# Weight sums and token splits moved in the order of a transform and dense-layer kernel

## The chip, the cores and the metric

The kernel runs on one core of one Trainium2 chip. The metric is the device time of one execution in microseconds (us). TensorE is called PE here, VectorE DVE, ScalarE ACT, GpSimd POOL, and the queue that issues most transfers SP, as in the profile.

## The reference

What is computed is attention over 4 x 8 heads of 576 rows with a bias from a small network on the distance of two rows, then on its output `x` (4 batches, 576 rows, 512 columns) the real part of a Fourier transform over rows and columns, a normalisation and two dense layers:

```python
attn = exp(scores - max) / (sum + 1e-9);  x = attn @ v          # heads joined: (4, 576, 512)
X = np.fft.fft(np.fft.fft(x, axis=1), axis=2)
u = x + np.real(X)
un = (u - mean(u)) / np.sqrt(var(u) + 1e-6)
return u + np.maximum(un @ w_ch1, 0.0) @ w_ch2                  # 512 -> 2048 -> 512
```

## The kernel before

Each float32 operand of the dense layers and of the transform is kept as a high part (a copy rounded to a shorter mantissa, written by ACT) and a low part (the rest, a subtraction on DVE or POOL). A product is three matmul passes: high by high, high by low, low by high (`PROD`, L606). So every operand that reaches PE costs one ACT copy and one subtraction first (`split`, L936; `split_sum`, L1166).

Work is tiled in 128 rows. After attention, batches 0 and 1 run through `dense` (L948): for each of 16 slices f of the hidden layer, `layer(f)` (L987) makes the parts of the two weights, multiplies the tokens by the first weight (`up`, L966, into a PSUM tile `hp`) and makes the parts `hh` and `hl` of the positive part (`relu_parts`); `down(f)` (L995) multiplies by the second weight and adds into `acc`. Of the 30 pieces of batch 1, `main[-1]` is `layer(15)`, `main[-2]` is `down(13)`, and `last_down` is `down(14)` and `down(15)`.

While batch 1 runs, batches 2 and 3 are transformed in a list of steps (`BETWEEN`, L74). Letters are looked up in `step` (L1356): `f12` is the last feature transform (matmuls into the two PSUM tiles `abp`), `i12` an ACT copy of one of them (`bs`), and `j12` (`join`, L708) the last sums, two DVE instructions that write `dm` (L713) and `dp` (L714) from the other. `w` calls `pr.weights(0)` (L1171), see below. The lower half of `x` is added from `dm` by POOL (L727), the upper from `dp` by DVE (L724).

Batches 2 and 3 then run as a pair (`class Pair`, L1108) with a seven-product scheme in the style of Strassen: sums of tokens (operands "3" to "7", `second_low`, L1157) times sums of weights. `weights(i)` loads two weight slices into a room of its own, makes four sums on DVE (L1180, tiles `ws`), and returns `weight_parts(i)` (L1188), which splits them: ACT copies `w1h` (L939), `wo` (L1200 twice, L1204) and POOL subtractions (L940, L1201 twice, L1205). `split_sum` makes the parts of one token sum, 128 x 1024 elements: an ACT copy (L1168) and a subtraction on the engine named in its call (L1169). `product(i, n, bank)` (L1208) issues six matmuls into bank a, b, x or y; a and b take their PSUM buffers from the pool `hps`, of two buffers, which also holds `hp` of `up(14)` and `up(15)`. `product(0, "1", "a")` takes the first of them again and `product(0, "6", "b")` the second.

What sets the order: at this stage PE is in the order written (`manual_schedule(engines={PE_})`, L1384), and so is DVE (L899, to the end). ACT, POOL and SP are ordered by a planner at build time, which simulates the program, and gives an idle engine the ready instruction that stands first in the program. In `first_layers` (L1259) four ACT instructions have a written order of their own among themselves: the copy of bank a (L1268), then the high parts of "5", "7" and "4".

In the block at L1384 PE runs `main[-10]`, the first flips (transposes `ut`, L1125, into the pool `fps` of two buffers, which `abp` also used) of row tiles 0 and 1, `main[-9]`, the flips of tiles 2 and 3, and so on. On DVE, between them, stand the statistics (`stats`, L761) and `first_low` (L1135), which frees the flips' buffers.

Of the kernel before, what the change touches and what calls it, by code (L numbers as in the profile page):

```python
# [13 lines left out]
AF = mybir.ActivationFunctionType  # L14
# [60 lines left out]
p000 p001 p002 g00 p010 h00 z000 z001 a000 a001 p011 p012 g01 b000 b001 h01 z010 z011 a010 a011  # L75
p100 p101 p102 g10 b010 b011 f00 i00 h10 p110 j00 l00 k00 f01 i01 p111 p112 g11 j01 l01 k01 h11
z100 z101 a100 a101 m00 m01 b100 b101 z110 z111 a110 a111 m02 m03 b110 b111 f10 i10 r0 d00 d01
j10 f11 i11 l10 k10 d02 d03 R j11 f12 i12 l11 k11 w j12
""".split()


# [56 lines left out]
def body(ctx, tc, a, out):  # L138
    nc = tc.nc
# [68 lines left out]
    def prep(n):  # L208
        q, k = ld.pop(n)
        qs = stp.tile([P, 2 * S], F32R, tag="qs", name="qs")  # L210
        kh = stp.tile([P, KW], F32R, tag="kh", name="kh")
        kl = stp.tile([P, KW], F32R, tag="kl", name="kl")
        stk[n] = (qs, kh, kl)

        def hi(dst, src, c):
            if n < 2:
                nc.scalar.activation(dst[:, c], src[:, c], AF.Copy)
            else:
                nc.gpsimd.tensor_scalar(dst[:, c], src[:, c], 1.0, 0.0, ALU.mult, ALU.add)  # L219

        def lo(dst, src, ref, rows, c):
            eng = nc.vector if n < 2 else nc.gpsimd
            eng.tensor_tensor(dst[rows, c], src[rows, c], ref[rows, c].bitcast(F32), ALU.subtract)  # L223

        every, low = slice(0, 128), slice(64, 128)
        ca, cb, ck = slice(0, S), slice(S, 2 * S), slice(S, KW)
        return [
            lambda: hi(qs, q, ca), lambda: lo(qs, q, qs, low, ca),
            lambda: hi(kh, k, ca), lambda: lo(kl, k, kh, every, ca),
            lambda: hi(qs, q, cb), lambda: lo(qs, q, qs, low, cb),  # L230
            lambda: hi(kh, k, ck), lambda: lo(kl, k, kh, every, ck),
        ]
# [93 lines left out]
    with ExitStack() as st:  # L326
# [51 lines left out]
        ps = None  # L378
# [16 lines left out]
        for n, (u, t4, rev, low, _) in enumerate(steps):  # L395
# [13 lines left out]
            if t4 == 0:  # L409
                ps = bps.tile([P, 2, 512], F32, tag="ps", name="bps")  # L410
# [15 lines left out]
    with ExitStack() as st:  # L426
# [137 lines left out]
        PE_, DVE_, ACT_, POOL_ = (getattr(mybir.EngineType, e) for e in ("PE", "DVE", "Activation", "Pool"))  # L564
# [23 lines left out]
        for n in range(U - 1):  # L588
            pr = prep(n + 1) if n else []
# [35 lines left out]
        class Mix:  # L625
# [95 lines left out]
            def add(self, t, upper):  # L721
                for pr, bo, bi, tt, lo, hi in self.d[t]:
                    if upper:
                        nc.vector.tensor_tensor(  # L724
                            x[pr, bo, tt, 257:512], x[pr, bi, tt, 257:512], hi[pr, 255:0:-1], ALU.add)
                    else:
                        nc.gpsimd.tensor_tensor(x[pr, bo, tt, 0:257], x[pr, bi, tt, 0:257], lo[pr], ALU.add)  # L727
# [91 lines left out]
        n = U - 1  # L819
# [82 lines left out]
        for w in TAIL:  # L902
            u = n - w.count("'")
            w = w.rstrip("'")
# [20 lines left out]
        def w1_pair(j):  # L925
            return w1p.tile([P, 2, 4 * P], F32, tag=f"w1_{(j + 3) % 8}", name="w1")
# [6 lines left out]
        def w1_load(f, dst=None):  # L933
            nc.sync.dma_start(w1[f] if dst is None else dst, w1_d[f].rearrange("p k c -> p (k c)"))
# [173 lines left out]
        class Pair:  # L1108
# [150 lines left out]
            def first_layers(self, last_down):  # L1259

                add = lambda d, p, q: nc.vector.tensor_tensor(d, p, q, ALU.add)
                ps = self.ps = {}
                u2 = rawp.tile([P, 2, 512], F32, tag="raw", name="us")
                c21 = rawd.tile([P, 2, 512], F32, tag="raw", name="us")
                last_down[0]()
                self.product(0, "1", "a")
                with tc.manual_schedule(engines={ACT_}):
                    nc.scalar.activation(u2[:, 0], ps["a"], AF.Copy)  # L1268
                    for n, eng in (("5", nc.vector), ("7", nc.gpsimd), ("4", nc.gpsimd)):
                        self.split_sum(n, eng)  # L1270
                self.product(0, "6", "b")
                add(u2[:, 0], ps["b"], u2[:, 0])
                last_down[1]()
                self.product(0, "5", "y")
                self.product(0, "7", "x")
                add(u2[:, 1], ps["x"], u2[:, 0])
                self.product(0, "2", "a")
                add(self.hc[1], ps["y"], u2[:, 1])
                self.weights(1)[1]()
                self.halves(0, ps["a"])  # L1280
                self.product(0, "4", "x")
                add(c21[:, 0], ps["x"], u2[:, 0])
                self.product(0, "3", "y")
                add(self.hc[0], ps["y"], u2[:, 0])
                self.w2_get(0)
                self.halves(1, c21[:, 0])
# [65 lines left out]
        pr = Pair(2)  # L1352
# [27 lines left out]
        def each(fn, *ts):  # L1380
            for t in ts:
                fn(t)

        with tc.manual_schedule(engines={PE_}):  # L1384
            main[-10]()
            each(first, 0, 1)
            each(stats, 0, 2)
            each(pr.first_low, 0, 1)
            main[-9]()
            each(first, 2, 3)  # L1390
            each(stats, 1, 3)
            each(pr.first_low, 2, 3)
            main[-8]()
            main[-7]()
            root()
            each(scale, 0, 1, 2, 3)
            pr.late_rooms()
            main[-6]()
            main[-5]()
            parts[1]()  # L1400
            each(flip, 0, 1)
            each(pr.second_low, 0, 1)
            mx[1].add(2, False)
            mx[1].add(2, True)
            main[-4]()
            main[-3]()
            each(flip, 2, 3)
            each(pr.second_low, 2, 3)
            pr.upper_parts(0, parts[0])
            main[-2]()  # L1410
            pr.split_sum("6", nc.vector)
            main[-1]()
            pr.run_first(last_down, end)
            un, stats, root, scale = norm(rest_tiles, lambda: pp.tile([P, 2, 512], F32, tag="p", name="un", bufs=4))
            room = []

            def rest_flip(t):
                if not room:
                    room.append(pp.tile([P, 2, 4, 256], F32R, tag="p", name="uo", bufs=4))
                ps = tps.tile([P, 4, P], F32, tag="t", name="ut")  # L1420
                c = slice(P * t, P * t + P)
                for kb in range(4):
                    nc.tensor.transpose(ps[:, kb], un[0][:, t, P * kb:P * kb + P], ident)
                h, l = room[0][:, 0, :, c], room[0][:, 1, :, c]
                nc.scalar.activation(h, ps, AF.Copy)
                nc.vector.tensor_tensor(l, ps, h.bitcast(F32), ALU.subtract)

            def w1_again(j):
                t = w1_pair(j)
                for e in range(2):  # L1430
                    w1[2 * j + e] = t[:, e]
                    w1_load(2 * j + e)

            extra = {f: [lambda j=f - 2: w1_again(j)] for f in range(2, 10)}
            for f, p in ((3, lambda: stats(0)), (4, lambda: stats(1)), (5, root), (6, lambda: scale(0)),
                         (7, lambda: scale(1)), (10, lambda: rest_flip(0)), (11, lambda: rest_flip(1))):
                extra.setdefault(f, []).append(p)
            pr.run_second(extra)
# [69 lines left out]
```

## Time and profile before

| what | us |
|---|---|
| median of the timed runs | 757.22 |
| fastest timed run | 757.07 |
| the profiled execution, whole | 757.49 |
| its span, first to last instruction | 755.7 |
| around the span (757.49 - 755.7) | 1.8 |

A row of the timeline gives the start, the time taken, engine and line, operation, output and inputs, the shape, how many instructions were merged (x), and in brackets how long the engine stood idle before it and what ended that.

### The profile page before, as it was taken

Reading aid. Unit: us, or ns where it says so; the run is one execution under the profiler, and the core shown is the slowest. Engines: PE = TensorE matmul, PEld = TensorE weight load, DVE = VectorE, ACT = ScalarE, POOL = GpSimd, SP = SyncE. Lnnn points to the kernel's source line nnn. Section 1 sums busy time; section 2 is a strip of 40 time slices with the busy share of each in tenths; the row PEclk is TensorE's granted clock in tenths of the full one; section 3 lists DMA queues with packets and bytes.
Section 4 is the critical chain, followed back from the end, with each engine's and each line's share of the span. In section 5 each row is a group of like instructions: output and inputs, shape, how many; then the busy total and the mean of one; then the engine's idle time right before and its main releaser. Section 6 shows DMA issues by size and latency. Waiting matters only on the chain.

```text
span 755.7 us, 13307 instructions
## 1 busy us (share of the span) xinstructions
PE 738.5 (98%) x4731; PEld 602.5 (80%) x4731; DVE 489.3 (65%) x1044; ACT 440.2 (58%) x912; POOL 347.6 (46%) x301
## 2 busy tenths in 40 slices
PE   6999999999999999999999999999999999999998
PEld 3567787888878888878888888878878888888897
DVE  7997584787687887794866476666474433354433
ACT  7997888788888788753333343344533342344453
POOL 0002654754465754125464445366864353344442
PEclk9999999999999999999999999999999999999999
DMA  8988889679479882265532221212242223642432
GB/s 220 240 218 210 197 228 277 184 198 299 124 205 255 240 263 84 89 207 170 167 112 84 61 80 29 69 38 62 70 140 58 69 83 98 204 152 78 139 91 78
DMA packets 62771, 110.85 MB, mean 147 GB/s; under 512 B 9232, under 2 KB 28304, under 8 KB 61584
## 3 DMA queue, kind: packets, MB, share of 16 engines
q1 hardware_dynamic: 58976, 102.13, 47.2%
q10 hardware_dynamic: 3440, 4.78, 1.9%
q0 software_dynamic: 288, 3.08, 1.1%
q8 instruction: 37, 0.61, 0.3%
q14 instruction: 30, 0.25, 0.1%
HBM read 86.24 MB, written 21.07 MB: 142 GB/s over the span
## 4 chain that ended last, share of the span: by engine, by line
PE 87%; ACT 4%; DMA 3%; SPq 2%; issue 1%; DVE 1%; POOL 1%; ACTq 0%; DVEq 0%; POOLq 0%
PE acc L999 14%; PE hp L974 14%; PE acc L1249 12%; PE s L282 11%; PE o L483 10%; PE t L462 8%; PE hpy L1218 3%; PE hpx L1218 3%; PE hpa L1218 3%; PE zp L681 2%; PE abp L701 2%; PE hpb L1218 1%; DMA bias<-ring 1%; ACT ha L390 1%; ACT ring L358 1%
## 5 line engine op out<-in xcount | busy, mean ns | idle before, releaser
L303 DVE CUSTOM_DVE_ANT_0 p<-s,bias 128x576 f32<-128x576 f32 x128 | 95.2, 754 | 54.9 <-PE s L282 50.0
L940 POOL TENSOR_TENSOR w2l<-w2f,w2h 128x512 fp32r<-128x512 f32 x64 | 85.1, 1329 | 92.5 <-ACT w2h L939 92.3
L940 POOL TENSOR_TENSOR w1l<-w,w1h 128x512 fp32r<-128x512 f32 x55 | 72.7, 1322 | 70.4 <-ACT w1h L939 68.1
L282 PE MATMUL s<-kh,qs 128*128 128x288 f32 (+1 forms) x320 | 98.2, 326 | 1.8 <-DVE nm L303 1.8
L442 ACT ACTIVATE pt<-t 128x512 f32<-128x512 f32 x141 | 77.8, 594 | 37.6 <-PE t L462 20.1
L318 ACT ACTIVATE p<-p,nm 128x576 f32<-128x576 f32 x128 | 98.0, 769 | 2.6 <-DVE nm L303 2.6
L282 PE MATMUL s<-kl,qs 128*128 128x288 f32 (+1 forms) x320 | 88.0, 294 | 0.8 <-DVE kl L223 0.8
L483 PE MATMUL o<-pt,v 128*64 128x288 f32 x640 | 84.2, 411 | 0.0
L219 POOL TENSOR_SCALAR kh<-kT 128x576 fp32r<-128x576 f32 (+1 forms) x28 | 20.7, 758 | 137.3 <-PE s L282 117.9
L939 ACT ACTIVATE w2h<-w2f 128x512 fp32r<-128x512 f32 x80 | 50.2, 627 | 56.1 <-PE acc L999 22.4
L462 PE MATMUL t<-ident,p 128*128 128x128 f32 x576 | 78.9, 273 | 0.7 <-ACT pt L442 0.7
L983 DVE SCALAR_TENSOR_TENSOR hl<-hp,hh 128x512 fp32r<-128x512 f32 (+1 forms) x48 | 28.9, 601 | 75.7 <-ACT hh L982 75.5
L939 ACT ACTIVATE w1h<-w 128x512 fp32r<-128x512 f32 x55 | 34.7, 632 | 65.8 <-PE hp L974 48.6
L282 PEld LDWEIGHTS s<-kh,qs 128*128 128x128 f32 (+1 forms) x320 | 58.5, 183 | 18.1 <-issue 7.4
L483 PEld LDWEIGHTS o<-pt,v 128*64 128x64 f32 x640 | 43.2, 137 | 30.8 <-issue 4.5
L462 PEld LDWEIGHTS t<-ident,p 128*128 128x128 f32 x576 | 66.5, 140 | 1.6 <-ACT pt L442 1.4
L999 PE MATMUL acc<-w2h,hh 128*128 128x512 f32 x160 | 62.7, 393 | 0.0
L999 PE MATMUL acc<-w2l,hh 128*128 128x512 f32 x160 | 62.4, 391 | 0.0
L282 PEld LDWEIGHTS s<-kl,qs 128*128 128x128 f32 (+1 forms) x320 | 58.8, 184 | 1.0 <-DVE kl L223 1.0
L999 PE MATMUL acc<-w2h,hl 128*128 128x512 f32 x160 | 59.5, 391 | 0.0
L412 PE MATMUL bps<-hd,sm 128*32 128x288 f32 x432 | 50.9, 420 | 7.5 <-DVE hd L392 5.3
L1249 PE MATMUL acc<-w2h,hh 128*128 128x512 f32 x128 | 50.0, 391 | 0.0
(200 smaller groups left out, 1771.6 us busy)
## 6 DMA issues: line engine op xcount, KB each, us to landing
w2f<-w_d SPq DMA_DIRECT2D x80, 256.0 KB, 2.6
raw<-m SPq DMA_DIRECT2D x24, 512.0 KB, 4.8
w<-w_d SPq DMA_DIRECT2D x45, 256.0 KB, 3.4
kT<-kT SPq DMA_DIRECT2D x32, 304.0 KB, 5.1
qT<-qT SPq DMA_DIRECT2D x32, 288.0 KB, 4.3
bias_d<-ring SPq DMA_DIRECT2D x54, 144.0 KB, 2.7
bias<-bias_d SPq DMA_DIRECT2D x24, 288.0 KB, 5.2
v<-v SPq DMA_DIRECT2D x16, 320.0 KB, 5.7
```

The lines of the kernel that those rows point to most:

```text
L282: nc.tensor.matmul(ps[:m, c, :CH], qs[:, c0:c0 + m], kk[:, k0 + c * CH:k0 + (c + 1) * CH], start=k == 0, stop=k == 1, skip_group_check=True)
L303: nc.vector.tensor_tensor_reduce(p, bank.pop((n, i))[:, :, :CH], bias, -0.125, 3.0e38, ALU.add, ALU.min, nms[n][:, blk:blk + 1])
L318: nc.scalar.activation(p, p, AF.Exp, bias=nms[n][:, blk:blk + 1], scale=-1.0, accum_out=sums[n][:, blk:blk + 1])
L442: nc.scalar.activation(dst, src, AF.Copy)
L462: nc.tensor.transpose(tp[:, 128 * t:128 * t + 128], pb[t].rearrange("p h s -> p (h s)")[:, k0:k0 + 128], ident)
L483: nc.tensor.matmul(os_[u][e, c, :CH], vt[u][:, j, e], pts[u][:, 2 * j + h if j < 4 else 8, c * CH:(c + 1) * CH], start=j == 0, stop=j == 4 ...
L939: nc.scalar.activation(h, src, AF.Copy)
L940: eng.tensor_tensor(l, src, h.bitcast(F32), ALU.subtract)
L974: nc.tensor.matmul(ps[:, :N], w[wi][:, P * kb:P * kb + P], ut[ui][:, kb, :N], start=i == 0, stop=i == len(mm) - 1)
L999: nc.tensor.matmul(acc[t], h[i][:, P * t:P * t + P], w[j], start=f == 0 and k == 0, stop=f == NF - 1 and k == 2)
L1218: nc.tensor.matmul(self.ps[bank], w[wi][:, P * kb:P * kb + P], u[ui][:, kb], start=first and k == 0, stop=k == len(mm) - 1, skip_group_che ...
L1249: nc.tensor.matmul(self.acc[t], h[i][:, P * t:P * t + P], w[j], start=f == 0 and k == 0, stop=f == NF - 1 and k == 2)
```

## The change

Three moves. In the list `BETWEEN`, `j12` (the transform's last sums) goes ahead of `w` (the first weight sums of the pair). The splits of token sums "7", "5" and "4" leave `first_layers` and stand behind that of "6", ahead of `main[-1]`, in the program order 6, 7, 5, 4; the written order of ACT goes with them. And `self.weights(1)[1]()`, which loads, sums and splits the second weights, goes from behind product "2" to behind product "6", ahead of `down(15)`.

```diff
-j10 f11 i11 l10 k10 d02 d03 R j11 f12 i12 l11 k11 w j12
+j10 f11 i11 l10 k10 d02 d03 R j11 f12 i12 l11 k11 j12 w
...
                 self.product(0, "1", "a")
-                with tc.manual_schedule(engines={ACT_}):
-                    nc.scalar.activation(u2[:, 0], ps["a"], AF.Copy)
-                    for n, eng in (("5", nc.vector), ("7", nc.gpsimd), ("4", nc.gpsimd)):
-                        self.split_sum(n, eng)
+                nc.scalar.activation(u2[:, 0], ps["a"], AF.Copy)
                 self.product(0, "6", "b")
                 add(u2[:, 0], ps["b"], u2[:, 0])
+                self.weights(1)[1]()
                 last_down[1]()
                 self.product(0, "5", "y")
                 self.product(0, "7", "x")
                 add(u2[:, 1], ps["x"], u2[:, 0])
                 self.product(0, "2", "a")
                 add(self.hc[1], ps["y"], u2[:, 1])
-                self.weights(1)[1]()
                 self.halves(0, ps["a"])
...
             pr.split_sum("6", nc.vector)
+            pr.split_sum("7", nc.gpsimd)
+            pr.split_sum("5", nc.vector)
+            pr.split_sum("4", nc.gpsimd)
             main[-1]()
             pr.run_first(last_down, end)
```

## Rows read from the trace of the kernel before

**Rows 1.** The page's first part: busy time, share of the span, instructions.

```profile
PE 738.5 (98%) x4731; PEld 602.5 (80%) x4731; DVE 489.3 (65%) x1044; ACT 440.2 (58%) x912; POOL 347.6 (46%) x301
```

**Rows 2.** Waits of PE, whole span: waiter, releaser, us in total, times, longest.

```profile
PE ut L1125 <- DVE dp L714: 1.2, 1, 1.2
...
PE hpx L1218 <- POOL wo L1201: 0.8, 1, 0.8
```

**Rows 3.** Timeline of all engines, 503 to 513 us.

```profile
505.17 0.74 DVE L1180 TENSOR_TENSOR ws<-w 128x256 f32<-128x256 f32 x1
...
506.06 0.60 PE L1125 MATMUL ut<-ident,un 128*128 128x128 f32 x4
...
506.96 0.48 DVE L713 SCALAR_TENSOR_TENSOR dm<-abp,dc,bs 128x257 f32<-128x257 f32 x1
...
507.01 1.27 POOL L940 TENSOR_TENSOR w2l<-w2f,w2h 128x512 fp32r<-128x512 f32 x1 [1.38 <-ACT w2h L939]
...
507.36 0.48 DVE L714 SCALAR_TENSOR_TENSOR dp<-abp,dc,bs 128x257 f32<-128x257 f32 x1
...
507.75 0.69 DVE L761 BATCH_NORM_STATS2 bn<-x 128x6 f32<-128x512 f32 x1
...
507.89 0.66 PE L1125 MATMUL ut<-ident,un 128*128 128x128 f32 x4 [1.24 <-DVE dp L714]
...
508.24 1.57 POOL L727 TENSOR_TENSOR x<-x,dm 64x257 f32<-64x257 f32 x2
...
509.36 1.59 DVE L1135 TENSOR_TENSOR uo<-ut,uo 128x256 fp32r<-128x256 f32 x4
...
509.89 2.54 POOL L1201 TENSOR_TENSOR wo<-ws,wo 128x512 fp32r<-128x512 f32 x2
...
511.15 1.03 PE L1125 MATMUL ut<-ident,un 128*128 128x128 f32 x8
```

**Rows 4.** Line 1180, all 16 of one form: duration in ns, min/median/max.

```profile
L1180 DVE TENSOR_TENSOR ws<-w x16: 409/418/887, 505.2 to 633.9; 128x256 f32<-128x256 f32 x16
```

**Rows 5.** Timeline of all engines, 547 to 556 us: the second weight sums.

```profile
547.33 1.31 POOL L940 TENSOR_TENSOR w2l<-w2f,w2h 128x512 fp32r<-128x512 f32 x1
...
548.03 0.89 DVE L1180 TENSOR_TENSOR ws<-w 128x256 f32<-128x256 f32 x1
...
548.58 1.49 POOL L940 TENSOR_TENSOR w1l<-w,w1h 128x512 fp32r<-128x512 f32 x1
...
548.96 1.40 DVE L1180 TENSOR_TENSOR ws<-ws,w 128x256 f32<-128x256 f32 x1
...
551.97 1.67 PE L1218 MATMUL hpb<-uo,wo 128*128 128x512 f32 x6
...
555.89 0.39 PE L1218 MATMUL hpy<-uo,wo 128*128 128x512 f32 x1
```

**Rows 6.** Timeline of all engines, 532.5 to 545.5 us: token splits, layer 15.

```profile
533.15 0.63 ACT L939 ACTIVATE w2h<-w2f 128x512 fp32r<-128x512 f32 x1 [2.17 <-issue]
...
533.68 1.04 ACT L1168 ACTIVATE uo<-us 128x1024 fp32r<-128x1024 f32 x1
...
534.82 2.37 DVE L1169 TENSOR_TENSOR uo<-us,uo 128x1024 fp32r<-128x1024 f32 x1 [1.42 <-POOL us L1163]
...
534.82 1.29 POOL L940 TENSOR_TENSOR w2l<-w2f,w2h 128x512 fp32r<-128x512 f32 x1
...
537.12 0.68 DVE L983 SCALAR_TENSOR_TENSOR hl<-hp,hh 128x512 fp32r<-128x512 f32 x1
...
539.70 1.52 PE L1218 MATMUL hpb<-uo,wo 128*128 128x512 f32 x6
...
541.28 0.39 PE L999 MATMUL acc<-w2l,hh 128*128 128x512 f32 x1
...
541.53 1.23 DVE L1169 TENSOR_TENSOR uo<-us,uo 128x1024 fp32r<-128x1024 f32 x1 [3.74 <-ACT uo L1168]
...
542.59 2.43 POOL L1169 TENSOR_TENSOR uo<-us,uo 128x1024 fp32r<-128x1024 f32 x1 [2.05 <-ACT uo L1168]
```

## What the change should do: the prediction

> **What bounds the kernel now.** I read the page's busy row first: PE is busy for 738.5 us, 98% of the span, and no other engine passes 65% [rows 1]. So time is won only where PE stands still, and lost only where PE is made to. Next the waits of PE: behind the attention there are two left that the change touches, 1.2 us for `dp` and 0.8 us for the split weight sums `wo` [rows 2]. No edit here takes work off PE or adds any, so the most that can be won is these two gaps; the timeline around each gives their full size. Four transposes (`ut`) start at 506.06 and the next four only at 507.89; the later eight, from 511.15, take about 0.8, 0.4 for four, so the second four could have started at 506.46 and the first gap is 1.43 [rows 3]. Second, in `layers(1)` product "6" (`hpb`) starts at 551.97 and product "5" (`hpy`), two products later, at 555.89: 3.92 for what takes 2 x 1.36 undisturbed (six matmuls at the pitch (1.52 - 0.39) / 5 = 0.226 of the product at 539.70), so the second gap is 1.20 [rows 5, 6]. Together 2.6 us, 0.35% of the time. A measurement of this kernel can tell about 2%, some 15 us, from no change; so by that bound the answer is no change, and the question is the sign of one or two microseconds.
>
> **Part A, `j12` ahead of `w`.** On DVE the four weight sums take 505.17 to 506.96, then `dm` and `dp` follow, and `dp` is done at 507.84; PE starts 0.05 later [rows 3]. Swapped, `dm` starts at 505.17, `dp` at 505.57 and ends at 506.05, before PE wants the buffer (506.46). That wait goes. What is late next: PE reaches the flips of tiles 2 and 3 at 511.15 - 1.43 = 509.72, and these need the buffers that `first_low` of tiles 0 and 1 frees on DVE. DVE runs without a gap through sums, statistics and `first_low` until 509.36 + 1.59 = 510.95 [rows 3], and a swap doesn't shorten that row of work. So how much of the 1.43 stays is set by how long the four sums take in their new place, from 505.96 on.
>
> Alone, a sum takes 0.418 [rows 4]; the four, at the pitch that 1.79 for them shows less the 0.32 by which the first is over 0.418, take 1.47 [rows 3, 4]. But where POOL works on SBUF operands at the same time they wait: the first of the second weights took 0.89 beside a `w2l`, the next 1.40, and the `w1l` between the two was stretched from 1.3 to 1.49 [rows 5]. The ends (548.64, 548.92, 550.07, 550.36) come one behind the other, in the order in which the four asked: one at a time. The Trainium skill, page "SBUF — State Buffer", section "SBUF: two separate sides", says the same: DVE with two SBUF inputs and GpSimd take turns at one pair of ports as an exclusive lock, held for the whole instruction, the loser fully blocked. The trace agrees (1.40 for 0.42). By that rule part A comes out as in the third case below; with no such rule it would be the first, and the whole sum 755.1.
>
> Three ends. First, no meeting: the sums end at 507.43, statistics (507.75 to 509.36, 1.61) at 509.04, `first_low` of tile 0 at 509.84 and of tile 1 at 510.63. The fourth flip starts then; before it started at 511.15 + 0.40 = 511.55: 0.92 won. Second, only the `w2l` of 507.01 gets ahead of the fourth sum: that sum ends about 508.6, `first_low` of tile 1 at 511.8: 0.25 lost. Third, the two POOL sums L727 come too. They need only `dm`, and `dm` is now ready at 505.65, in a stretch in which POOL stands idle for 1.38 until 507.01; the planner fills an idle engine, so they move ahead of `w2l` [rows 3]. Then, one at a time: L727 505.70 to 506.48 (half of 1.57), sum 1 to 506.73 (0.25 of port each), L727 to 507.51, sum 2 to 507.76, `w2l` to 509.05, sum 3 to 509.30, sum 4 to 509.60; statistics to 511.2, `first_low` of tile 1 to 512.8: 1.25 lost. If one `wo` split (half of 2.54) also slips in ahead of sum 4, 2.5. Bounds: 0.92 won to 2.5 lost. I take 1.25 lost, since the idle 1.38 is there and nothing but `dm` holds L727 back.
>
> **Part B, the splits ahead of layer 15.** PE waits for none of them now, so nothing is won here at once; their room is used by part C. ACT: three copies of 1.04 come some 6 us earlier, into a stretch where it has idle time (2.17 before 533.15) [rows 6]. POOL: two subtractions of 2.43 come ahead. DVE: the low part of "5" now stands, in the written order, ahead of `hl` of layer 15, and behind `hl` queue the sums after products "6", "7" and "5". Product "6" can't start before `hl` has read its buffer. Today `hl` ends at 537.80 and the product starts at 539.70: slack 1.90 [rows 6]. The subtraction of "5" takes 1.23 alone: hidden. At the 2.37 that "6" took beside POOL it overruns by 0.47; with a whole 2.43 of POOL in front of its 1.23, by 1.76 [rows 6]. I take 0.3, between nothing and 0.47, since `w2l` of 534.82 would still be first on POOL.
>
> **Part C, second weights sooner.** Its two loads (SP) go into a room that is free long before, and the planner has issued them early as it is; the sums move past nothing on SP that PE waits for. The four sums start about 542, after product "6", instead of 548.03 [rows 5, 6]; the splits of ACT and POOL follow some six us sooner, which covers the 1.20 even if each sum waits for one POOL instruction of 1.3 (5.2). The wait goes whole: 1.20 won. The DVE sums that used to queue behind them, for products "7" and "5", still have their place, since `hpx` comes only 4 us after `hpb`.
>
> **Sum.** 1.25 + 0.3 - 1.20 = 0.35 longer: 757.49 + 0.35 = 757.84 for the profiled execution, whose 1.8 around the span I leave alone. The median stands 0.27 below it, so 757.6.
>
> **The rivals.**
> *Both waits go* (faster). The planner leaves L727 where it is and the sums slip between POOL's instructions: 0.92 + 1.20 = 2.1 won, 755.1; with the whole first gap, 754.6. For it: both gaps are plain in the waits, and DVE has nothing else urgent. Against: POOL's next ready work is L727.
> *Layer 15's second weight comes late* (slower). ACT copies "5", "6", "7" and "4" ahead of `w2h` of layer 15, since they now stand first in the program, and POOL then subtracts "7" and "4" ahead of `w2l`. Today `w2l` ends at 536.11 and PE reads it at 541.28: slack 5.17 [rows 6]. In front of it come 2 x 2.43 of POOL and, taking turns, 2 x 1.23 of DVE: 7.3, so 2.15 late. It decides from the point where both POOL subtractions go first; one alone costs nothing. Sum 1.25 + 2.15 - 1.20 = 2.2 longer: 759.4. For it: the planner's rule. Against: today it issued `w2h` (533.15) ahead of the copy of "6" (533.68), although that one stands earlier in the program, so the weight was ready first [rows 6].
> *The splits don't move* (the change fails to do what it says). With no written order ACT copies "5" behind the copy of bank a, as now; but DVE's order holds `hl` behind it: "5" is split at 541.53 to 542.76, `hl` ends near 543.4, product "6" waits 3.7 [rows 6]. Sum 3.8 longer, 761.0. ACT's idle time speaks against it.
>
> **How the numbers follow.** Forecast (waits gone, about the same given back): 0.42; its own range, with A between 0.25 and 1.25 and B between 0 and 0.47, is 756.3 to 757.8. Both waits go: 0.25. Late second weight: 0.28. Splits not moved: 0.05. Cases of both signs hold much of the chance, so the range spans them: from 755.0 to 759.7, which leaves out the whole gap won (0.04), A at its 2.5 together with a late weight (0.08) and the last case (0.05). No case comes near 15 us: within 2% 0.98, faster 0.01 and slower 0.01 for a plan turned over as a whole.
>
> **What would show it.** Right on A: `dp` ends near 506.05, no wait of PE for it, L727 ahead of `w2l` on POOL, weight sums of 0.6 to 1.3 instead of 0.42, and a new PE wait for `first_low` (L1135) near 511. Right on B: `hl` of layer 15 ends between 539 and 540.2 and PE loses under half a microsecond at `hpb`. Right on C: no wait of `hpx` for `wo`. Wrong: PE waits for `w2l` at `down(15)` (the late weight), or no PE wait behind 506 at all (both go).

## The result, and the profile after

The changed kernel takes 762.80 us, the median of 7 runs (759.95 to 763.28); the kernel before took 757.51 beside it. The ratio is 1.0056, with a 95% interval from 1.0037 to 1.0075: 5.3 us slower, where 757.6 was forecast, and above the range's upper end of 759.7. Two repeats of the same kernel gave 1.0061 [1.0047, 1.0075] and 1.0059 [1.0043, 1.0074]. By the bound of 2% it is still "within". The profiled execution took 759.96, with a span of 758.2. It is one of the shorter ones: it lies 2.5 above the profiled execution before, less than half of the timed difference.

The busy row of the page after, which answers to [rows 1]:

```profile
PE 740.6 (98%) x4731; PEld 605.1 (80%) x4731; DVE 494.3 (65%) x1044; ACT 440.4 (58%) x912; POOL 349.7 (46%) x301
```

Every engine's row counts as many instructions as before, and PE is busy 2.1 us longer. The same matmuls took longer, so something beside waiting has changed. The waits of PE after, from 500 to 700 us, answer to [rows 2]:

```profile
PE ut L1125 <- DVE uo L1135: 3.1, 1, 3.1
PE hpx L1218 <- DVE us L1261: 0.6, 1, 0.6
```

Both old waits are gone, as forecast, and two new ones stand in their place. The wait for `dp` (1.2) has become a wait of 3.1 for `first_low` (L1135), and the wait for `wo` (0.8) one of 0.6 for a DVE sum. The timeline after around the first weight sums, 504 to 514 us, answers to [rows 3] and [rows 4] (start, length, engine, line; in brackets the wait ahead):

```profile
504.72 0.48 DVE L714 SCALAR_TENSOR_TENSOR dp<-abp,dc,bs 128x257 f32<-128x257 f32 x1
504.88 1.61 POOL L727 TENSOR_TENSOR x<-x,dm 64x257 f32<-64x257 f32 x2
505.11 0.79 DVE L1180 TENSOR_TENSOR ws<-w 128x256 f32<-128x256 f32 x1
505.21 1.03 PE L1125 MATMUL ut<-ident,un 128*128 128x128 f32 x8
505.93 0.85 DVE L1180 TENSOR_TENSOR ws<-ws,w 128x256 f32<-128x256 f32 x1
506.58 1.36 POOL L940 TENSOR_TENSOR w2l<-w2f,w2h 128x512 fp32r<-128x512 f32 x1
506.70 1.51 DVE L1180 TENSOR_TENSOR ws<-w 128x256 f32<-128x256 f32 x1
507.89 1.47 POOL L1201 TENSOR_TENSOR wo<-ws,wo 128x512 fp32r<-128x512 f32 x1
508.14 1.50 DVE L1180 TENSOR_TENSOR ws<-w,ws 128x256 f32<-128x256 f32 x1
509.57 0.68 DVE L761 BATCH_NORM_STATS2 bn<-x 128x6 f32<-128x512 f32 x1
511.17 1.40 DVE L1135 TENSOR_TENSOR uo<-ut,uo 128x256 fp32r<-128x256 f32 x4
512.05 1.94 PE L1125 MATMUL ut<-ident,un 128*128 128x128 f32 x8 [3.07 <-DVE uo L1135]
513.64 0.78 PE L999 MATMUL acc<-w2h,hh 128*128 128x512 f32 x1
```

All eight first flips now run in one go, 1.03 instead of two times 0.6 with a gap. But the four sums, 0.42 each when alone, take 0.79, 0.85, 1.51 and 1.50, one at a time with the POOL instructions: the two L727, `w2l`, and one `wo` split; the last two end 0.3 behind the ends of `w2l` and of the split. They last from 505.11 to 509.64. Statistics and `first_low` queue behind them, and PE stands still for 3.07. The next lines show the second effect: these eight flips take 1.94 instead of 1.03, and one matmul of L999 0.78 instead of the 0.39 of [rows 6]. The windows of the same trace (engine busy us and counts, then the granted clock, DMA share, GB/s) say why:

```profile
511.00:512.00 1.00, 0.00 (x0) 0.00 (x0) 0.97 (x5) 0.31 (x1) 1.00 (x2) 0.89 0.03 8
512.00:513.00 1.00, 0.95 (x5) 0.98 (x6) 1.00 (x3) 0.00 (x0) 0.88 (x1) 0.50 0.00 0
514.00:515.00 1.00, 1.00 (x3) 0.78 (x3) 0.97 (x3) 1.00 (x5) 0.00 (x0) 0.50 0.00 0
515.00:516.00 1.00, 1.00 (x5) 0.79 (x4) 0.91 (x4) 0.50 (x2) 0.00 (x0) 0.90 0.00 0
516.00:517.00 1.00, 1.00 (x6) 0.81 (x6) 0.28 (x1) 0.00 (x0) 0.00 (x0) 1.00 0.03 8
```

At the end of the wait the granted clock falls to 0.50, the 1.2 GHz level, and is back at 1.00 (2.4 GHz) in the window from 516.

The timeline after around layer 15 and the second weight sums answers to [rows 5] and [rows 6]:

```profile
536.02 0.61 ACT L939 ACTIVATE w2h<-w2f 128x512 fp32r<-128x512 f32 x1
537.23 1.31 POOL L940 TENSOR_TENSOR w2l<-w2f,w2h 128x512 fp32r<-128x512 f32 x1
537.67 3.64 DVE L1169 TENSOR_TENSOR uo<-us,uo 128x1024 fp32r<-128x1024 f32 x2 [1.86 <-POOL uf L1164]
541.23 0.68 DVE L983 SCALAR_TENSOR_TENSOR hl<-hp,hh 128x512 fp32r<-128x512 f32 x1
542.14 1.55 PE L1218 MATMUL hpb<-uo,wo 128*128 128x512 f32 x6
543.52 2.41 POOL L1169 TENSOR_TENSOR uo<-uf,uo 128x1024 fp32r<-128x1024 f32 x1
544.44 1.77 DVE L1180 TENSOR_TENSOR ws<-w 128x256 f32<-128x256 f32 x1
546.25 1.40 DVE L1180 TENSOR_TENSOR ws<-ws,w 128x256 f32<-128x256 f32 x1
547.57 1.51 DVE L1180 TENSOR_TENSOR ws<-w 128x256 f32<-128x256 f32 x1
549.00 1.51 DVE L1180 TENSOR_TENSOR ws<-w,ws 128x256 f32<-128x256 f32 x1
550.43 0.68 DVE L1261 TENSOR_TENSOR us<-hpx,us 128x512 f32<-128x512 f32 x1
551.16 1.66 PE L1218 MATMUL hpx<-uo,wo 128*128 128x512 f32 x6 [0.64 <-DVE us L1261]
```

`hl` of layer 15 ends at 541.91, 0.23 before product "6" starts, and PE doesn't wait there. The four second sums again collide with POOL (1.77, 1.40, 1.51, 1.51), and the sum behind product "7" (L1261), queued behind them, reaches DVE only at 550.43, so PE waits 0.64.

### The profile page after: what moved, and what is told of

Its sections match the earlier page's. It is cut to its first block, busy times and chain, and to the rows that moved or that the text cites. A ratio compares the mean times of both kernels' runs of the same rounds, so it can differ in the third digit from the quotient of the medians.

```text
span 758.2 us, 13301 instructions
## 1 busy us (share of the span) xinstructions
PE 740.6 (98%) x4731; PEld 605.1 (80%) x4731; DVE 494.3 (65%) x1044; ACT 440.4 (58%) x912; POOL 349.7 (46%) x301
## 4 chain that ended last, share of the span: by engine, by line
PE 91%; DVE 4%; ACT 2%; DMA 1%; issue 1%; ACTq 0%; DVEq 0%; SPq 0%
PE acc L999 14%; PE hp L974 14%; PE s L282 12%; PE acc L1249 12%; PE o L483 10%; PE t L462 8%; PE bps L412 4%; PE hpx L1218 3%; PE hpy L1218 3%; PE hpa L1218 3%; PE zp L681 2%; PE abp L701 2%; PE hpb L1218 1%; DVE ws L1180 1%; PE t L452 1%
## 5 line engine op out<-in xcount | busy, mean ns | idle before, releaser
L999 PE MATMUL acc<-w2h,hh 128*128 128x512 f32 x160 | 63.1, 396 | 0.0
L999 PE MATMUL acc<-w2l,hh 128*128 128x512 f32 x160 | 62.7, 393 | 0.0
L999 PE MATMUL acc<-w2h,hl 128*128 128x512 f32 x160 | 59.7, 393 | 0.0
L1249 PE MATMUL acc<-w2h,hh 128*128 128x512 f32 x128 | 50.0, 391 | 0.0
```

The lines of the kernel that those rows point to most:

```text
L999: nc.tensor.matmul(acc[t], h[i][:, P * t:P * t + P], w[j], start=f == 0 and k == 0, stop=f == NF - 1 and k == 2)
L1249: nc.tensor.matmul(self.acc[t], h[i][:, P * t:P * t + P], w[j], start=f == 0 and k == 0, stop=f == NF - 1 and k == 2)
```

## The experiments

PE's work ahead of the first flip is the same in every kernel here, yet that flip starts anywhere from 504.72 to 508.71 in the traces. So the traces are compared by stage: from the start of the first flip (the first L1125 of [rows 3]) to the third flip's start, to the first matmul of product "1" (`hpa`, bank a, the start of `layers(1)`), and to the first `down` matmul of L1249 (557.26 before); the tail is the span less that matmul's start. A is `j12` ahead of `w`, B the early splits, C the earlier second weights. The offsets are worked out from start times in the timelines; the ratio is the timed one against the kernel before on the same chip, and 95% intervals stand with each experiment.

| kernel | 3rd flip | bank a | first down | tail | time | ratio |
|---|---|---|---|---|---|---|
| before | 5.09 | 32.28 | 51.20 | 198.44 | 757.5 | 1 |
| before, again (b_look) | 5.07 | 32.26 | 51.20 | 198.49 | 757.67, one | |
| after, A+B+C | 6.84 | 35.56 | 54.27 | 198.72 | 762.80 | 1.0056 |
| after again (r_after) | 6.84 | 35.71 | 54.38 | 199.48 | 763.06 | 1.0061 |
| after again (r2_after) | 6.83 | 35.57 | 54.27 | 199.53 | 762.47 | 1.0059 |
| after again (r3_after) | 6.85 | 34.32 | 53.01 | 199.49 | 760.70, one | |
| after again (r4_after) | 6.84 | 35.85 | 54.54 | 198.63 | 761.99, one | |
| e1: A | 6.84 | 35.67 | 54.59 | 198.45 | 760.91 | 1.0048 |
| e2: B | 5.09 | 32.28 | 50.64 | 198.44 | 757.83 | 1.0000 |
| e3: C | 5.08 | 32.26 | 56.21 | 199.50 | 763.53 | 1.0069 |
| e4: B+C | 5.09 | 32.28 | 51.00 | 198.65 | 757.92 | 1.0004 |
| e5: A, L727 on DVE | 4.97 | 32.43 | 51.35 | 198.46 | 758.15 | 1.0008 |
| e6: A+B+C, wait filled | 6.86 | 34.30 | 53.01 | 199.56 | 759.55 | 1.0027 |
| e7: sums behind `first_low` | 3.64 | 34.94 | 53.88 | 198.47 | 760.09 | 1.0033 |
| e8: e7+B | 3.64 | 33.29 | 51.71 | 198.48 | 760.21 | 1.0030 |
| e9: sums ahead of `f12` | 3.64 | 30.83 | 49.75 | 198.42 | 756.37 | 0.9989 |
| e10: e9+B | 3.61 | 30.83 | 49.24 | 198.45 | 755.58 | 0.9968 |
| e11: e9+B+C | 3.64 | 30.83 | 49.53 | 199.58 | 757.00 | 0.9988 |

**Part A alone.**

```diff
-j10 f11 i11 l10 k10 d02 d03 R j11 f12 i12 l11 k11 w j12
+j10 f11 i11 l10 k10 d02 d03 R j11 f12 i12 l11 k11 j12 w
```

> Only j12 ahead of w; the splits and the second weights stay as before. Theory 1 (turn-taking at the swap): the first weight sums meet POOL's L727, w2l and wo, first_low comes late, PE waits about 3 us for L1135 near 512 and its clock falls afterwards as in the changed kernel; the second gap of 1.2 stays. Time 760 to 764, mean granted clock 0.995 to 0.998. Theory 2 (the loss is made by the splits and the second weights): no new wait that is longer than 1.2, time 757.5 or less.

Measured: 760.91 against 757.36, ratio 1.0048 [1.0035, 1.0060]. Its waits of PE hold the new wait and the old one for `wo`:

```profile
PE ut L1125 <- DVE uo L1135: 3.0, 1, 3.0
PE hpx L1218 <- POOL wo L1201: 0.8, 1, 0.8
```

Bank a comes 3.39 later than before, the timed runs are 3.55 longer. So A alone carries most of the loss.

**Parts B and C without A**: the change's other two hunks, with `w j12` left as it was.

> The changed kernel with w ahead of j12 again (splits early and second weights sooner stay). Theory 1: the 3 us wait and the fall of the clock are gone, the wait for dp of 1.2 is back; the second gap shrinks from 1.2 to the 0.6 wait of hpx; time 756.5 to 757.5, clock 1.0. Theory 2: 759 or more.

Measured: 757.92 against 757.36, ratio 1.0004 [0.9995, 1.0013]; the stage to the first down is 0.20 shorter. The wait that is left is `PE hpx <- DVE us`, 0.7. With A taken back the loss is gone, and B and C together move next to nothing. The time lies 0.4 above the range expected, but its interval holds no change.

**A with its POOL meeting removed.** The two low sums L727 of that tile are put on DVE, in the same place in the program, so that POOL has no ready work there:

```diff
-            def add(self, t, upper):
+            def add(self, t, upper, eng=nc.gpsimd):
...
-                        nc.gpsimd.tensor_tensor(x[pr, bo, tt, 0:257], x[pr, bi, tt, 0:257], lo[pr], ALU.add)
+                        eng.tensor_tensor(x[pr, bo, tt, 0:257], x[pr, bi, tt, 0:257], lo[pr], ALU.add)
...
-            mx[1].add(2, False)
+            mx[1].add(2, False, nc.vector)
```

> The swap alone, with the two sums L727 of the last tile taken off POOL: DVE makes them, in the place of the list where the upper ones are made (about 527 us). The result is the same. Theory 1: only w2l and one wo split are left to take turns with the weight sums, so their four take about 3 us instead of 4.5 and PE's wait for L1135 falls from 3.1 to between 0.5 and 2; 757 to 760. Rival (the order on DVE alone makes the wait, whoever works on POOL): wait of 3 as in the swap alone, 760 to 764.

Measured: 758.15 against 757.36, ratio 1.0008 [0.9999, 1.0017]. Its timeline, first and fourth sum and the flips behind:

```profile
505.49 0.41 DVE L1180 TENSOR_TENSOR ws<-w 128x256 f32<-128x256 f32 x1
...
506.62 1.52 DVE L1180 TENSOR_TENSOR ws<-w,ws 128x256 f32<-128x256 f32 x1
...
510.56 1.29 PE L1125 MATMUL ut<-ident,un 128*128 128x128 f32 x8 [1.17 <-DVE uo L1135]
```

Three sums take 0.41 or 0.42, only the last meets `w2l` (1.52); the wait is 1.17 instead of 3.07, no fall of the clock follows, and 3.24 of e1's 3.39 at bank a are back. The collision with POOL is what makes A slow; the work of the sums isn't.

**The same wait, filled.** In the changed kernel the product of layer 11 (`up`) that runs ahead of the third flip is issued twice, the second time over the first result, so PE works where it waited. This repeats work and leaves none out.

```diff
-                mm = [(kb, i, j) for kb in range(4) for i, j in PROD]
+                mm = [(kb, i, j) for kb in range(4) for i, j in PROD] * (2 if f == 11 and n == 4 and not n_first else 1)
...
-                        start=i == 0, stop=i == len(mm) - 1)
+                        start=i % 12 == 0, stop=i % 12 == 11)
```

> The changed kernel, but the twelve matmuls of up(11) are issued twice (the second pass starts over in the same bank, so the result is the same): PE has 2.7 us more of work just where it would stand still for 3.1. Theory 1 with a clock share: PE's wait shrinks to about 0.4, the granted clock stays at 1.0, and the time falls by what the low clock costs, from 760-763 to 758-759. Rival (the low clock is a symptom that costs nothing beyond the wait): time as in the changed kernel or 0 to 0.5 longer, 760 to 763.

Measured: 759.55 against 757.36, ratio 1.0027 [1.0014, 1.0039], faster than the changed kernel although it does more, and just above the 758 to 759 expected. The third flip starts as late as in the changed kernel, but runs at the full clock, as does what follows:

```profile
512.99 1.29 PE L1125 MATMUL ut<-ident,un 128*128 128x128 f32 x8 [0.34 <-DVE uo L1135]
514.03 0.48 PE L999 MATMUL acc<-w2h,hh 128*128 128x512 f32 x1
```

Bank a comes at 34.30 instead of 35.56. So the loss at bank a has two terms: 34.30 - 32.28 = 2.02 from the late flips, and 1.26 from the clock that fell with PE idle ahead of it.

**Part B alone**: the three splits moved, ACT's written order dropped.

> Only the splits of 7, 5 and 4 ahead of layer 15, and no written order on ACT; w stays ahead of j12 and the second weights stay behind product 2. Theory 1 (the sums of the second weights only move from one meeting with POOL to another): with the splits out of the way POOL is nearly idle at 547, the second weight sums run at about 0.42 to 0.9 each, and PE's wait for wo (0.76, the gap of 1.20) shrinks or goes; 756.3 to 757.4. Rival (splits cost by themselves, hl of layer 15 comes late): a new PE wait at hpb of 0.5 to 1.8, 757.9 to 759.

Measured: 757.83 against 757.47, ratio 1.0000 [0.9989, 1.0011]. The stage from bank a to the first down is 18.36, against 18.92 before: 0.56 won in the trace; the timed runs, whose interval is wider than that, don't show it. Two of the four second sums still meet POOL (1.51 each), but the first `wo` split ends 13.15 behind bank a instead of 14.05. PE doesn't wait for the splits or for `hl`; the wait for POOL's `wo` (0.8) has become a shorter one for ACT's:

```profile
PE hpb L1218 <- ACT wo L1200: 0.4, 1, 0.4
```

**Part C alone**: `self.weights(1)[1]()` behind the sum of bank b, the splits left where they were.

> Only the second weights sooner; the splits of 5, 7 and 4 keep their written order on ACT behind the copy of bank a. My sum as predicted: the gap of 1.20 goes, stage 50.0, no wait of hpx. Theory 1 (turn-taking): the four sums meet the POOL subtractions of 2.43 and last 5 us or more, DVE comes late for the sums behind products 7 and 5 and PE waits at the next hpx for DVE instead: stage 50.8 to 53.

Measured: 763.53 against 757.46, ratio 1.0069 [1.0049, 1.0088], the slowest of all. A line of its waits of PE, then one of its windows, then three of its timeline:

```profile
PE hpx L1218 <- ACT wo L1200: 3.4, 1, 3.4
```

```profile
550.00:555.00 5.00, 3.77 (x9) 3.06 (x10) 3.16 (x5) 2.05 (x4) 3.44 (x4) 0.50 0.50 159
```

```profile
543.09 2.03 DVE L1180 TENSOR_TENSOR ws<-w 128x256 f32<-128x256 f32 x1
...
544.80 2.58 POOL L1169 TENSOR_TENSOR uo<-uf,uo 128x1024 fp32r<-128x1024 f32 x1
...
545.16 2.51 DVE L1180 TENSOR_TENSOR ws<-ws,w 128x256 f32<-128x256 f32 x1
```

Here POOL's token splits stand where the sums now come, and the first two sums take 2.03 and 2.51 beside them; `wo` is 3.4 late and the clock falls to 0.50 behind it. From bank a to the first down it takes 23.95 instead of 18.92. This is more than theory 1 expected, and the wait is for a split of the sums, not for DVE. So C needs B's room; with it (e4) it costs 0.36 more than B alone (51.00 against 50.64).

**The sums behind `first_low`.** A third place for the first sums: `w` taken out of the list, and issued behind `first_low` of all four tiles.

```diff
-j10 f11 i11 l10 k10 d02 d03 R j11 f12 i12 l11 k11 w j12
+j10 f11 i11 l10 k10 d02 d03 R j11 f12 i12 l11 k11 j12
...
             each(pr.first_low, 2, 3)
-            main[-8]()
+            main[-8](), parts.extend(pr.weights(0))
```

> j12 without w in front, as in the changed kernel, but w (the first weight sums) behind first_low of all four tiles instead of directly behind j12; nothing else of the change. Theory 1 (turn-taking of the weight sums with POOL, on DVE ahead of first_low, makes the wait): neither the wait for dp nor one for L1135; PE runs through from 505 to 552, the clock stays at 1.0; the first gap of 1.43 is won, 755.7 to 756.4. Rival (j12 in front is bad by itself, because L727 then comes early): a PE wait at L1135 of 1 or more, 757 to 760.

Measured: 760.09 against 757.47, ratio 1.0033 [1.0023, 1.0043]. The first gap goes whole: third flip at 3.64 instead of 5.09, that is 1.45, the 1.43 that the prediction read from [rows 3]. But 14 us behind the third flip PE waits 2.2 for `raw`, tokens that DVE scales (L785) with a factor `rs` that it had late; so neither theory came. Three lines of its timeline:

```profile
519.30 1.00 DVE L767 SCALAR_TENSOR_TENSOR rs<-mv 128x4 f32<-128x4 f32 x1
...
521.58 1.20 DVE L771 SCALAR_TENSOR_TENSOR rs<-rs 128x4 f32<-128x4 f32 x1
...
524.53 1.54 PE L1154 MATMUL ut<-ident,raw 128*128 128x128 f32 x8 [2.21 <-issue]
```

These DVE operations of 128x4, whose medians in this trace are 0.17 (L771) and 0.27 (L767), take this long beside whole POOL instructions of 1.3: parts of the pair's weights (`w1l`, `wo`), which follow the later sums, and a `w2l` at 521.47 behind them. The first `raw` then takes 1.40 instead of 0.53 and ends at 524.43, 0.1 ahead of the flip; the trace names no releaser for this wait, so this is read from the order of times. The granted clock is 0.50 behind it, from 526 to 528, and the stage ends 2.68 later than before.

**The same with B.**

> The same with the splits of 7, 5 and 4 ahead of layer 15 as well; the second weights stay behind product 2. Theory 1: both gaps are won or nearly so, no PE wait over 0.4 between 505 and 654; 754.6 to 755.8. Rival (the splits cost by themselves): as the kernel with the late first sums or up to 1.5 longer.

Measured: 760.21 against 757.47, ratio 1.0030 [1.0019, 1.0041]. The same wait of 2.2 stands in its waits, but this profiled execution shows no fall of the clock there, and bank a comes at 33.29 instead of 34.94. It shows one elsewhere: in the attention, behind a wait of 1.76 that ends at 124.40, the granted clock is 0.50 from 126 to 128. No other trace here has that fall, and this one has the latest first flip (508.71): of the 3.2 us that this execution took more than the profiled one before, 2.65 lie ahead of the stage.

**The changed kernel again.**

> The changed kernel once more beside the others, on this chip. Its first runs lay at 760 and at 763 with a mean granted clock between 0.998 and 0.995. If the low clock behind the 3 us wait lasts for a varying time, the runs spread over 760 to 763.5 again and the longer ones show the lower mean clock; if the spread was of the chips, they lie within 1 us of each other here.

Measured: 763.06, ratio 1.0061 [1.0047, 1.0075]; wait, fall and stage as in the first trace. Its six runs on one chip spread from 760.83 to 763.32, so the spread is not of the chips.

**The sums earlier instead of later.** `w` is put ahead of `f12`, into a stretch in which DVE stood idle for 4.46 us in the trace before, ahead of `hl` of layer 10, and `j12` is alone behind `k11`.

```diff
-j10 f11 i11 l10 k10 d02 d03 R j11 f12 i12 l11 k11 w j12
+j10 f11 i11 l10 k10 d02 d03 R j11 w f12 i12 l11 k11 j12
```

> j12 without w in front, and w (the first weight sums) earlier than before, ahead of k11, where DVE has 4.5 us without work behind it; nothing else of the change. Theory 1 (only the place in which the weight sums and POOL take turns decides): no wait of PE from the first flip to layer 15, the clock stays up, the stage from the first flip to the first down of the pair shrinks from 51.20 to 49.8; 755.5 to 756.5. Rival (a flip of row tiles needs the slack that the wait for dp gave, and a later wait takes its place, as with the late first sums): stage 51 or more, 757 or more.

Measured: 756.37 against 757.46, ratio 0.9989 [0.9978, 0.9999]. Bank a comes 1.45 earlier: the whole first gap, and nothing given back.

> The same with the splits of 7, 5 and 4 ahead of layer 15. Theory 1: the second gap shrinks by 0.56 as with the splits alone (stage 50.64 against 51.20), on top of 1.4: stage 49.2, time 754.8 to 756. Rival (the first sums' parts now stand elsewhere on POOL and the two gains don't add): stage 49.8 or more.

With B as well: 755.58 against 757.46, ratio 0.9968 [0.9955, 0.9980], the fastest version found, 1.9 us below the kernel before; the stage is 1.96 shorter. Three lines of its timeline show that the collisions are still there:

```profile
497.28 0.80 DVE L1180 TENSOR_TENSOR ws<-w 128x256 f32<-128x256 f32 x1
...
499.22 1.51 DVE L1180 TENSOR_TENSOR ws<-w,ws 128x256 f32<-128x256 f32 x1
...
503.52 0.68 DVE L983 SCALAR_TENSOR_TENSOR hl<-hp,hh 128x512 fp32r<-128x512 f32 x1
```

Sums of 0.80 and 1.51 as in the changed kernel, but they and the two sums L724 behind them, slowed as well, fit into what was idle time: the `hl` behind starts 1.39 ahead of the first flip (504.91), where it started 1.50 ahead of it before. So the collisions cost nothing. The only wait of PE listed for its trace from 480 us on is the 0.4 for ACT's `wo`.

> The first weight sums early (ahead of k11), the splits ahead of layer 15, and the second weights sooner as in the change: only the place of w differs from the changed kernel. Theory 1 (turn-taking): no wait for L1135 and no low clock; the second weights sooner still make PE wait 0.6 to 0.7 at hpx for DVE, so the stage is 49.2 + 0.4 = 49.6, and the time 755.8 to 757.2. Rival (the second weights sooner are worth their gap of 1.2 once the first part is mended): stage 48.5 to 49, 754.5 to 755.5.

With C on top (e10 + C): 757.00 against 757.84, ratio 0.9988 [0.9979, 0.9997]. The stage is 0.29 longer than e10's, the tail 1.13.

**Repeats for the clock and the tail.** The changed kernel three times more, the kernel before once:

> The changed kernel a third time. Its stage from the first flip to the first down of the pair was 54.27 and 54.38, the kernel before had 51.20, so 3.1 is the change's own; of the 2.9 between the two executions 2.0 lay ahead of the first flip and 0.8 behind the first down, where both run the same work. If that is chance, runs lie between 759.9 and 763.4 again and the stage is 54.3 in whichever is profiled; if the change makes a second state, the stage itself is longer in a long run.

> The changed kernel, one more trace. Open is why its runs lie at 760 to 761 or at 763. Chance ahead of the first flip: the stage is 54.3 again and the first flip starts anywhere between 504.7 and 508.7, as in the other kernels. A cause in the change: the tail behind the first down of the pair is 198.7 or 199.5, where kernels without the second weights sooner have 198.4 to 198.5.

> As the run before: stage 54.3; first flip by chance between 504.7 and 508.7; tail 198.7 or 199.5 if the second weights sooner lengthen it.

> The kernel before, one more trace beside these, for the same three parts: stage 51.2, tail 198.4, first flip between 504.7 and 508.7.

Measured: 762.47 (ratio 1.0059 [1.0043, 1.0074]), and one profiled execution each of 760.70, 761.99 and, for the kernel before, 757.67. In r3_after PE waits as long as ever and yet the clock doesn't fall: a matmul of L999 takes 0.47 there, and 0.77 in r4_after, each behind the same wait. Two lines of r3_after's timeline, then two of r4_after's:

```profile
513.25 1.29 PE L1125 MATMUL ut<-ident,un 128*128 128x128 f32 x8 [3.05 <-DVE uo L1135]
...
514.29 0.47 PE L999 MATMUL acc<-w2h,hh 128*128 128x512 f32 x1
```

```profile
513.87 1.75 PE L1125 MATMUL ut<-ident,un 128*128 128x128 f32 x8 [3.07 <-DVE uo L1135]
...
515.27 0.77 PE L999 MATMUL acc<-w2h,hh 128*128 128x512 f32 x1
```

So one execution of the five traced was without the fall, and its stage (53.01) is that of e6, where the wait was filled: two ways to the same full-clock value. The five differ in all three parts: the first flip starts at 505.21 to 507.24, the stage is 53.01 or 54.27 to 54.54, and the tail is 198.63 to 199.53.

## Why the prediction was wrong

It forecast that the old waits go and that a new one for `first_low` comes, and so it was. It had that new wait too short, it left out the clock behind it, and it did not see the wait for the DVE sum in part C. It forecast no change; the change costs 5.3 us. By its own steps:

**What bounds the kernel: right but for the clock.** PE's gaps decide, and the first gap of 1.43 is 1.45 when it goes alone (e7, e9). Of the second gap of 1.20 no run won more than 0.56. The sentence that time is "lost only where PE is made to" stand still does not hold: PE also lost time at work, at the lower clock.

**Part A: right in kind, too small.** L727 ahead of `w2l`, sums one at a time with POOL, `first_low` late, a new wait of PE for L1135: all as described. The value taken, 1.25, was the third case; what came was the case beyond it, "if one `wo` split also slips in ahead of sum 4, 2.5", visible as the POOL L1201 of 507.89 beside the sum of 508.14. Two of the four sums were longer than the 0.6 to 1.3 it named as a sign. At full clock A costs 34.32 - 32.28 = 2.04 by r3_after, 2.02 by e6. The step that failed is "I take 1.25 lost", which counted only the POOL work that was ready when the sums begin, not what the first sums themselves make ready: `wo` is the split of the sums' own results. On the taking of turns the Trainium skill, page "SBUF — State Buffer", section "SBUF: two separate sides", says that the loser is blocked for the other's whole instruction; the trace agrees, with 1.50 for a sum of 0.42 beside a POOL instruction of 1.47.

**A term that was missing: the clock.** The prediction priced every wait at its own length. The wait of 3.07 is followed by about 3 us at the granted level 0.50, which cost 1.24 to 1.53 more at bank a (35.56 to 35.85 in four traces of the changed kernel, against 34.32 without the fall), and 1.35 in e1. It also goes with PE's busy time, which grew by 2.1 against [rows 1]: the four traces with the fall have 740.0 to 740.6, r3_after without it 738.4. With it A costs 3.3 to 3.6, not 1.25.

**Part B: -0.56 instead of +0.3.** POOL kept `w2l` of layer 15 first, `hl` ended 0.23 ahead of product "6", and the whole cost was hidden (its end, 541.91, less the 2.44 by which product "6" starts later, is 539.47, within the 539 to 540.2 it named as a sign). What the prediction left out is the gain: with ACT's and POOL's token splits out of the way, the splits of the second weights come sooner, and half of the second gap went with B alone (e2; again 0.51 from e9 to e10).

**Part C: +0.3 instead of -1.20.** The wait of `hpx` for `wo` went, as forecast. The step that failed is 'The DVE sums that used to queue behind them, for products "7" and "5", still have their place'. The prediction allowed each sum 1.3 of waiting for the splits' sake, but didn't carry the same 5.2 to the DVE queue behind. The sums took from 544.44 to 550.51, the sum behind product "7" started at 550.43, and PE waited 0.64 for it. From bank a to the first down the changed kernel takes 18.71, against 18.92 before: 0.21 won in B and C together, where 0.9 was forecast; e2 shows that B without C would have won 0.56.

**The tail.** All nine traces with C show a longer tail (198.63 to 199.58) than all nine without it (198.42 to 198.49), though the last matmuls stand at the same distance from the first down. In the DMA part of the trace of r2_after, 750 us to the end (the instruction queue, then the last stores with the us from issue to landing), stand two lines that differ from those before:

```profile
q14 instruction: 1, 0.01, 0.1%
...
out<-x ACTq DMA_DIRECT2D x2, 128.0 KB, 2.5
```

Before, the last instruction fetch lies at 748.5, 7.2 ahead of the end, and the same stores take 1.9; in r2_after it lies at 758.4, 2.3 ahead of the end. So it is in all 18 traces: with C the last fetch is 1.4 to 2.3 ahead of the end and the stores take 2.0 to 2.5, without C it is 7.1 to 7.5 ahead and they take 1.9. Among the nine with C the tail goes with the store (198.63 to 198.72 at 2.0 or 2.1, 199.48 to 199.58 at 2.5). That the fetch delays the store was not tested, nor does 0.6 explain the whole of up to 1.1. So 0.2 to 1.1 us of C's cost is located, not explained.

**The sum as measured.** A at full clock 2.04, the clock 1.2 to 1.5, B and C -0.2, the tail 0.2 to 1.1: 3.2 to 4.4. The traced executions agree: the five of the changed kernel took 761.6 in the mean, 4.0 more than the two of the kernel before. The timed difference of 5.3 is larger. About 1 us of it is found neither in the stages nor in the tail; the first flip starts at 506.56 in the mean of the five traces of the changed kernel and at 506.20 in that of the 13 others, within a scatter of 4. What it is stays open. Against the forecast, the terms that were off most are C (1.5), the clock (1.2 to 1.5) and A (0.8); B's gain of 0.9 hid part of it.

**The rivals and the range.** None of the three came. "Both waits go" failed at POOL's ready work, as the text against it said; what it promised (754.6 to 755.1) is what e10 reached by another placement (755.58). Layer 15's second weight wasn't late: `w2h` came at 536.02 and `w2l` at 537.23, ahead of both POOL token splits (540.18 and 543.52). The splits did move. The range ended at 759.7 because its slow end added up waits at their own length. A at its 2.5 bound would still have lain inside it with B and C as forecast (758.8); the clock and the tail, 1.4 to 2.6 together, and a loss in C were not in any case.

## What to carry to other kernels

Before DVE work with two SBUF inputs is moved, list the POOL instructions that are ready at the new place and those that the moved work itself releases, allow one whole POOL instruction for each, and carry that sum to everything queued behind on DVE; put such work where DVE is idle ahead of nothing urgent, as e9 and e10 do, and the same collisions are free. A wait of PE of about 3 us should be priced with the clock behind it, here 40 to 50% more. Two edits that are each harmless or useful may need each other (C without B cost 5 us in the stage), so cost them one by one and together.

## What was unexpected of the hardware

A wait of 3.0 to 3.1 us of PE was followed by the granted clock 0.50 in five of the six traces that have it (after four times, e1) and not in the sixth (r3_after); the one of 3.4 (e3) was followed by it; the wait of 2.2 was in e7 and not in e8, though in that same trace of e8 a wait of 1.76 was; behind the waits of 1.2 (before, e5) it never fell. So the length of the wait alone does not tell, and the same kernel has a chance element of 1.2 to 1.7 us at each such wait. DVE operations of 128x4, 0.17 and 0.27 in the median, took 1.00 and 1.20 when a POOL instruction of 1.3 was under way (e7): small operations paid for most of the other's length as well.
